# Sparse attention and gated feed-forward on one core: a first unit of 512 rows in the place of one of 384, with lent tiles, late mask copies and constant matmuls

## The chip, the core and the metric

The kernel runs on one NeuronCore of a Trainium2 chip. A core has five engines that run side by side: TensorE (PE: matmuls; PEld is its loading of weights), VectorE (DVE), ScalarE (ACT), GpSimd (POOL) and SyncE (SP, which here only issues DMA transfers). Sixteen DMA engines move data between HBM and the core's memory. Matmul results land in PSUM[...]; everything else lies in SBUF. The metric is the time in microseconds (us) of one execution on the device, as the median of several.

## The reference

Four batches of eight heads with 768 positions and 64 values a head pass a sparse causal attention. The keys are cut into 24 chunks of 32. For each query an upper bound of its score with each chunk is computed from the chunk's minimum and maximum; the six best chunks are kept. The attention's output, 3072 rows of 512, passes a feed-forward layer (FFN) with a sigmoid gate.

```python
ub = np.sum(np.maximum(q[:, :, :, None, :] * k_min[:, :, None, :, :], q[:, :, :, None, :] * k_max[:, :, None, :, :]), axis=-1)
ub = np.where(causal, ub, -1000000000.0)
top_chunks = np.argsort(ub, axis=-1)[..., -top_k:]
scores = scale * np.matmul(q, k.transpose(0, 1, 3, 2))
...
mask = sel & (pos[:, None] >= pos[None, :])
scores = np.where(mask, scores, -1000000000.0)
...
return np.matmul(attn, v)
# then, with x of 3072 x 512, w_gate and w_val 512 x 1536, w_out 1536 x 512:
gate = 1.0 / (1.0 + np.exp(-(x @ w_gate)))
val = x @ w_val
return gate * val @ w_out
```

## The kernel before

The rows are cut into 24 blocks of 128 (four batches of six). The first block of a batch sees at most four chunks, so all of them are kept and no choice is needed. A unit is a group of blocks that passes attention and FFN together. Each unit but the first is prepared (keys and queries turned, chunks chosen) and attended while PE also does the FFN of the unit before it.

```python
units = [
    Unit(0, [], [(0, 0), (1, 1), (2, 2)]),        # first blocks of batches 0, 1, 2
    Unit(1, [(0, 1), (0, 2), (0, 3)]),
    Unit(2, [(0, 4), (0, 5)], [(3, 2)]),          # and the first block of batch 3
    Unit(3, [(1, 1), (1, 2), (1, 3)]),
    ...
    Unit(7, [(3, 3), (3, 4), (3, 5)]),
]
```

A first block: its k and q are turned by PE (4 matmuls of 128x128 in f32 each), copied to f16, multiplied into scores, passed through exp on ACT, masked by a select on GpSimd, multiplied with the values, scaled and turned into `xT`, the FFN's input.

```python
def first(u, b, x, raw, base):
    for n in "kq":
        t = ps(f"{n}fT_{b}", "pr", [128, NP, 128])
        ...   # four transposes
        half[n] = Buf("np", f"{n}f16_{b}", [128, NP, 128], F16)
    ...
    val = Buf("np", f"vf_{b}", [128, H, D + 1], F16)
    att = [Buf("att", f"attf_{b}_{e}", [128, NP, 128], F16) for e in range(2)]
    ...   # scf (PE), expf (ACT), cmf (GpSimd select), pvf (PE), rzf and xf (DVE), xpsf (PE), xTf (DVE or ACT)
```

The FFN of a unit has twelve columns blocks `fb`. Each takes four matmuls for the gate, four for the value, a tanh on ACT (the sigmoid is made of it) and a product on DVE; then three row blocks of twelve output matmuls follow.

```python
def ffn(u, base, span):
    for fb in range(NFB):
        g = ps(f"g_{u.name}_{fb}", "ff", [128, T])      # T = 384
        w_ = ps(f"v_{u.name}_{fb}", "ff", [128, T])
        ...   # g: 4 matmuls, tanh on ACT; v: 4 matmuls, scalar_tensor_tensor on DVE
    for tb in range(3):
        ...   # o: 12 matmuls of 512 columns, a copy, a store
```

The FFN weights are loaded and cast to f16 by nine transfers issued by GpSimd (1 MB read each), the first pair after q of batch 1 has landed, the others after the last select of the first blocks:

```python
weights(0, -0.9, [(raw_f[1]["q"], 1)])
last = next(op for op in plan.ops if op.name == "cmf_2_1")
for i in range(1, 3):
    for op in weights(i, -0.5 + 0.2 * i, []):
        op.deps.append((last, False))
for i in range(3):
    weights_out(i, 0.3, []).deps.append((last, False))
```

A list scheduler inside the kernel (`Plan`) places every operation by a model of the engines, and the program is emitted in that order; each engine then runs its own instructions strictly in it. Constants in text (`NUDGES`, `LANDS`) steer it. They order instructions and are no waits on the chip.

Of the kernel before, what the change touches and what calls it, by code (L numbers as in the profile page):

```python
# [9 lines left out]
F16 = mybir.dt.float16  # L10
# [10 lines left out]
SHARED = {128: (0.145, 0.95), 256: (0.173, 0.90), 512: (0.22, 0.83), 768: (0.29, 0.78), 2048: (0.5, 0.5)}  # L21
SENT, LANDED = {SP: 700, POOL: 2700}, 1100
# [12 lines left out]
class Op:  # L35
    def __init__(self, name, engines, emit, prio, dma, rows, port):
        self.name, self.engines, self.emit, self.prio, self.dma = name, engines, emit, prio, dma
        self.rows, self.port = rows, port
        self.deps = []
        self.bufs = []  # L40
        self.start = self.done = self.engine = None

# [29 lines left out]
class Plan:  # L72
# [37 lines left out]
    def walk(self, land, prio=None, script=None, slow=1.0):  # L110
# [3 lines left out]
        line = {SP: 0.0, POOL: 0.0}  # L114
        port = {DVE: 0.0, POOL: 0.0}
        flight = []
# [4 lines left out]
        def inputs(op, e):  # L121
# [9 lines left out]
            for b in op.bufs:  # L131
                if b.kind == "ps":
                    for (other, r), done in seen.get(b, {}).items():
                        if other != e and r in op.rows:
                            t = max(t, done + HOP[e])
            if e == POOL:
# [28 lines left out]
        def place(op, e, s):  # L165
# [5 lines left out]
            if op.dma is not None:  # L171
                work = op.dma[0] * slow
                begin = max(line[e], s + SENT[e])
# [3 lines left out]
                if e == SP:  # L177
# [42 lines left out]
        while avail:  # L220
            best = None
            at = {}
            for op in avail:
# [3 lines left out]
                for e in op.engines:  # L227
                    at[op, e] = max(r, inputs(op, e))
# [27 lines left out]
    def landings(self, out, slow=1.0):  # L256

        queues = {SP: [], POOL: []}
        for op in out:
            if op.dma is not None:  # L260
                queues[op.engine].append([op.start + SENT[op.engine], op.dma[0] * slow, op])
# [3 lines left out]
        while queues[SP] or queues[POOL]:  # L265
# [5 lines left out]
            if len(on) == 2:  # L271
# [21 lines left out]
    def order(self):  # L293

        nudge = {n: int(x) for n, x in (w.rsplit(":", 1) for w in NUDGES.split())}
        lands = {n: float(x) for n, x in (w.rsplit(":", 1) for w in LANDS.split())}
        prio = {op: op.prio + nudge.get(op.name, 0) * 0.01 for op in self.ops}
# [7 lines left out]
ident:370 epat0:-92 epat:-143 kcr0:-70 kcr1:88 hq0:-119 hq1:74 ap0:168 v10:48 hkp000:102 hkp001:162 hkp010:1  # L305
hkp011:-53 ap1:113 v11:43 hkp100:139 hkp101:127 hkp110:-301 hkp111:-12 ident16:15 kf0_0:-159 kf1_0:-55 qf0_0:-66
qf1_0:-51 vf_0:27 kf0_1:-30 kf1_1:-16 qf0_1:-8 qf1_1:65 vf_1:10 kf0_2:24 kf1_2:41 qf0_2:-23 qf1_2:-11 vf_2:54
k0_u1:-125 k1_u1:-15 k2_u1:-44 k3_u1:35 q0_u1:-10 q1_u1:29 q2_u1:-4 q3_u1:38 v_0_1:-51 v_0_2:-11 v_0_3:24 kfT_0:99
kf16_0:-28 kxf0:60 kxf1:201 kcr_f:18 hkf0:348 hkf1:-115 qfT_0:94 qf16_0:-40 v16_0_0:238 scf_0:-96 expf_0_0:-210
# [998 lines left out]
```

The softmax here doesn't subtract the row's maximum and nothing guards it: scores larger than these inputs give would overflow.

## Time and profile before

| | |
|---|---|
| median of 3 executions | 294.98 us (293.96 to 295.21) |
| span of the profiled execution | 293.9 us |
| granted PE clock, mean | 0.988 |
| PE busy | 278.2 us, 95% |
| ACT, DVE, POOL busy | 195.8, 189.2, 92.5 us |
| HBM read, written | 30.67 MB, 6.29 MB |
| the chain that ended last | PE 78%, DMA 10%, DVE 4% |

The span is the time from the first to the last instruction of the profiled execution; it is about a microsecond shorter than the measured time. Matmuls overlap in PE's pipeline, so their busy times add up to more than the work; the time from one start to the next is the better measure of what a matmul costs. A wait is put down to the event that came last before the instruction could start.

### The profile page before, as it was taken

How to read it: one execution, taken by the hardware profiler on the slowest of the kernel's cores; microseconds unless marked ns; L12 is line 12 of the kernel's file. 1: busy time of each engine (PE TensorE's matmuls, PEld its weight loads, DVE VectorE, ACT ScalarE, POOL GpSimd, SP SyncE). 2: the span in 40 equal slices, each digit the busy share in tenths (PEclk: the TensorE clock that was granted, in tenths of full speed). 3: DMA queues.
4: the chain of work that ended last, by engine and by line, in shares of the span. 5: the costliest groups of instructions: out<-in, count | busy, mean ns of one | idle time of the engine just before them, and what ended most of it. 6: DMA issues, size and time to landing. Idle time of an engine off the chain costs nothing.

```text
span 293.9 us, 6954 instructions
## 1 busy us (share of the span) xinstructions
PE 278.2 (95%) x2656; PEld 176.7 (60%) x2656; DVE 189.2 (64%) x560; ACT 195.8 (67%) x398; POOL 92.5 (31%) x162
## 2 busy tenths in 40 slices
PE   2879998999989999999999999999999999999994
PEld 2645555767664566556666667676565557655651
DVE  8375883996999289999999899654134124432420
ACT  7674757977984879458889898886563466323321
POOL 6681314933652337013326954213000011000000
PEclk9977999999999999999999999999999999999999
DMA  7999999999967999399997300001100110011002
GB/s 165 218 249 216 197 197 235 220 146 166 184 100 90 203 188 184 67 215 152 142 210 145 111 3 3 0 2 39 71 2 1 50 60 0 2 38 71 0 15 95
DMA packets 123233, 32.69 MB, mean 111 GB/s; under 512 B 111424, under 2 KB 120128, under 8 KB 123200
## 3 DMA queue, kind: packets, MB, share of 16 engines
q1 hardware_dynamic: 118448, 27.53, 53.1%
q0 software_dynamic: 4752, 4.72, 9.5%
q8 instruction: 21, 0.34, 0.5%
q14 instruction: 12, 0.10, 0.1%
HBM read 30.67 MB, written 6.29 MB: 126 GB/s over the span
## 4 chain that ended last, share of the span: by engine, by line
PE 78%; DMA 10%; DVE 4%; SPq 2%; POOL 2%; ACT 1%; issue 1%; ACTq 0%; DVEq 0%
PE o_u L1168 20%; PE v_u L1146 18%; PE g_u L1146 18%; PE sc_u L1063 11%; DMA wo<-in_moe_w_out_dram 9%; PE pv_u L1096 6%; PE ube_u L1002 2%; SPq L742 2%; PE xps_u L1123 2%; DMA qf<-in_q_dram 1%; DVE qf_u L969 1%; DVE kcr L787 1%; DVE kt L953 1%; ACT attf L857 1%; PE qfT L815 1%
## 5 line engine op out<-in xcount | busy, mean ns | idle before, releaser
L1074 ACT ACTIVATE att_u<-sc_u 128x512 f16<-128x512 f32 (+3 forms) x184 | 88.0, 549 | 13.9 <-PE sc_u L1063 13.1
L1158 DVE SCALAR_TENSOR_TENSOR hg_u<-gate_u,v_u 128x384 f16<-128x384 f16 x96 | 51.8, 544 | 53.8 <-PE v_u L1146 37.0
L1146 PE MATMUL g_u<-xT_u,wg 128*128 128x384 f16 x384 | 79.3, 330 | 0.0
L1146 PE MATMUL v_u<-xT_u,wv 128*128 128x384 f16 x384 | 78.8, 328 | 0.3 <-DMA wv<-in_moe_w_val_dram 0.3
L1154 ACT ACTIVATE gate_u<-g_u 128x384 f16<-128x384 f32 x96 | 47.6, 495 | 39.1 <-DVE hg_u L1158 21.5
L1168 PE MATMUL o_u<-wo,hg_u 128*128 128x512 f16 x288 | 68.0, 379 | 1.1 <-DMA wo<-in_moe_w_out_dram 1.1
L1080 POOL TENSOR_SCALAR_AFFINE_SELECT att_u<-att_u 128x384 f16<-128x384 f16 (+1 forms) x56 | 28.4, 512 | 99.0 <-ACT att_u L1074 98.2
L1146 PEld LDWEIGHTS <-wv 128*128 128x128 f16 x384 | 36.8, 98 | 23.5 <-issue 0.8
L1146 PEld LDWEIGHTS <-wg 128*128 128x128 f16 x384 | 36.5, 99 | 21.8 <-issue 1.5
L1168 PEld LDWEIGHTS <-hg_u 128*128 128x128 f16 x288 | 27.1, 98 | 28.7 <-issue 1.5
L1177 ACT ACTIVATE osb_u<-o_u 128x512 f32<-128x512 f32 x20 | 12.1, 603 | 26.7 <-PE o_u L1168 25.0
L1096 PEld LDWEIGHTS <-att_u 128*128 128x128 f16 x640 | 25.5, 98 | 4.7
L1096 PE MATMUL pv_u<-v,att_u 128*128 128x65 f16 x640 | 28.0, 193 | 0.0
L1063 PE MATMUL sc_u<-hqo,hko 128*128 128x128 f16 (+2 forms) x220 | 27.8, 243 | 0.1
L1063 PE MATMUL sc_u<-hqe,hke 128*128 128x128 f16 (+2 forms) x220 | 27.1, 243 | 0.2 <-ACT att_u L1074 0.2
L1063 PEld LDWEIGHTS <-hke 128*128 128x128 f16 x220 | 16.8, 98 | 5.7 <-issue 1.2
L779 POOL CAST v<-v 128x512 f16<-128x512 f32 x23 | 13.9, 619 | 19.2 <-DMA v<-in_v_dram 18.9
L1063 PEld LDWEIGHTS <-hko 128*128 128x128 f16 x220 | 16.3, 98 | 4.8 <-issue 0.2
L576 DVE COPY xT_u<-xps_u 128x384 f16<-128x384 f16 (+1 forms) x17 | 5.7, 338 | 14.4 <-PE xps_u L1123 14.3
L1115 DVE TENSOR_TENSOR x_u<-pv_u,rz_u 128x384 f16<-128x384 f32 (+1 forms) x28 | 14.5, 523 | 0.4
L1025 DVE MAX8 mx_u<-ubn_u 128x8 f32<-128x8 f32 (+16 forms) x152 | 12.4, 156 | 0.1
L787 DVE TRANSPOSE_TENSOR_REDUCE kcr<-k 128x24 f32<-128x768 f32 x12 | 11.2, 941 | 0.8 <-DMA k<-in_k_dram 0.8
(119 smaller groups left out, 306.9 us busy)
## 6 DMA issues: line engine op xcount, KB each, us to landing
out_dram<-osb_u SPq DMA_DIRECT2D x24, 256.0 KB, 2.4
v<-in_v_dram SPq DMA_DIRECT2D x23, 256.0 KB, 5.0
k<-in_k_dram SPq DMA_DIRECT2D x12, 384.0 KB, 6.1
q<-in_q_dram SPq DMA_DIRECT2D x12, 384.0 KB, 6.8
wg<-in_moe_w_gate_dram POOLq DMA_DIRECT2D x3, 512.0 KB, 10.2
wv<-in_moe_w_val_dram POOLq DMA_DIRECT2D x3, 512.0 KB, 12.8
wo<-in_moe_w_out_dram POOLq DMA_DIRECT2D x3, 512.0 KB, 23.3
kf<-in_k_dram SPq DMA_DIRECT2D x8, 128.0 KB, 3.6
```

The source lines that it names most:

```text
L779: plan.add(f"v16_{b}_{ib}", {POOL: pool(H * D)}, lambda e: nc.gpsimd.tensor_copy(v16[b % 2][:, ib, :, 0:D], at(t)), reads=[t], writes=[("v ...
L787: plan.add(f"kx{m}_{name}_{p}", {DVE: dve(size)}, lambda e, m=m, op=op: nc.vector.tensor_reduce(out=outs[m](), in_=src(), op=op, axis=AX.X ...
L1025: nc.vector.max(at(mx)[:, e_, j, :], at(ubn)[:, e_, j, 0:max(8, u.seen[j])])
L1063: nc.tensor.matmul(at(t)[:, o:o + 128 * m], hk[b % 2][e_][:, p, 128 * jb:128 * jb + 128], hq[u.side][e_][:, p, 128 * x:128 * (x + m)], sta ...
L1074: plan.add(f"exp_{u.name}_{h}_{y}", {ACT: act(n)}, lambda e, t=t, att=att, b0=b0, n=n: nc.scalar.activation(at(att)[:, b0:b0 + n], at(t), ...
L1080: nc.gpsimd.affine_select(out=dv, in_=dv, compare_op=ALU.is_ge, fill=0.0, base=0, pattern=[[0, u.m], [1, 128]], channel_multiplier=-1)
L1096: nc.tensor.matmul(at(pv)[:, last, x, :], at(att)[:, c:c + 128], v16[b % 2][:, jb, h, :], start=(jb == 0), stop=(jb == ib))
L1115: plan.add(f"x_{u.name}_{p}", {DVE: dve(u.t)}, lambda e: nc.vector.tensor_tensor(at(x_).rearrange("p a (e d) -> p e a d", e=2), at(pv)[:, ...
L1146: nc.tensor.matmul(at(t), w16[:, c, 128 * fb:128 * fb + 128], at(u.xt)[:, c, :], start=(c == 0), stop=(c == 3))
L1154: plan.add(f"tanh_{u.name}_{fb}", {ACT: act(T)}, lambda e, g=g, gate=gate: nc.scalar.activation(at(gate), at(g), AF.Tanh, scale=0.5), read ...
L1158: plan.add(f"hg_{u.name}_{fb}", {DVE: dve(T)}, lambda e, w_=w_, gate=gate, hg=hg: nc.vector.scalar_tensor_tensor(at(hg), at(gate), 1.0, at ...
L1168: nc.tensor.matmul(at(o), at(hgs[fc])[:, 128 * tb:128 * tb + 128], wo16[:, fc, :], start=(fc == 0), stop=(fc == NFB - 1))
```

## The change

Unit 0 takes the first blocks of all four batches, 512 rows, and unit 2 has only its two blocks of batch 0, 256 rows. The purpose is to have more FFN work at hand while the weights are still landing, and the first block of batch 3 out of the way of the later attention. What goes with it:

- The small tiles of the first blocks (k and q in f16, values, attention) are lent: they lie in the key, query and value buffers of later batches (`hk[1]`, `hq[0]`, `v16[1]`), and in the buffers `qm` and `qf` for the raw data of batches 2 and 3. The operations that write those buffers for their own purpose wait for the last use.
- The mask copies into `hk` (`hkp`) are held back until the first gate product of unit 0, or of unit 1 for the second buffer.
- Constant matmuls (identity times identity, about 55) are put into PE's gaps in the front, so that PE's clock stays up. Their result is not used.
- The FFN's matmuls take as many columns as the unit has rows (512, 256 or 384). In unit 0 four gate products come before the first four value products; in the others one.
- The weight transfers are chained one after another and wait for q of batch 2 instead of q of batch 1.
- The chosen chunks' tile `ubn` shares the one buffer of `qm`.
- An early exp on ACT loads its table; the scheduler's model is refined and has a new list `HOLDS`, which only moves operations in the order; all of `NUDGES` and `LANDS` is new.

```diff
-        Unit(0, [], [(0, 0), (1, 1), (2, 2)]),
+        Unit(0, [], [(0, 0), (1, 1), (2, 2), (3, 3)]),
         Unit(1, [(0, 1), (0, 2), (0, 3)]),
-        Unit(2, [(0, 4), (0, 5)], [(3, 2)]),
+        Unit(2, [(0, 4), (0, 5)]),
...
-                      reads=[epat], writes=[("hkp", i, e_, p) for p in range(o, NP, 2)], prio=0.3 + 0.2 * i, port=True)
+                      reads=[epat], writes=[("hkp", i, e_, p) for p in range(o, NP, 2)], prio=0.7 + 0.8 * i, port=True)
+                later.append((f"hkp{i}{e_}{o}", "g_u0_0" if i == 0 else "g_u1_0"))
...
-            half[n] = Buf("np", f"{n}f16_{b}", [128, NP, 128], F16)
+            half[n] = Lent(hk[1][b // 2], (0, 1024, 0, 1544)[b] + 512 * "kq".index(n), [NP, 128])
...
-            val = Buf("np", f"vf_{b}", [128, H, D + 1], F16)
+            val = Lent(*((None, None), (hk[1][0], 2048), (hk[1][1], 1024), (hq[0][0], 0))[b], [H, D + 1])
...
-        att = [Buf("att", f"attf_{b}_{e}", [128, NP, 128], F16) for e in range(2)]
+        att = [Lent(v16[1], 1024 * b - 1024 + 512 * e, [NP, 128]) if b else Buf("att", f"attf_{b}_{e}", [128, NP, 128], F16)
+               for e in range(2)]
...
-        ubn = Buf("ubn", f"ubn_{u.name}", [128, 2, u.nb, 32])
+        ubn = Buf("qm", f"ubn_{u.name}", [128, 2, u.nb, 32])
...
-            g = ps(f"g_{u.name}_{fb}", "ff", [128, T])
+            g = ps(f"g_{u.name}_{fb}", "ff", [128, u.rows])
...
+        first_ = 4 if u.i == 0 else 1
+        for fb in range(first_):
+            gated(fb)
+        for fb in range(first_):
+            valued(fb)
+        for fb in range(first_, NFB):
+            gated(fb)
+            valued(fb)
...
-        for tb in range(3):
+        for tb in range(u.rows // 128):
...
+    warm = ps("warm", "wm", [128, 128])
+    for name, n in {"": 10, "kfT_0": 4, "qfT_0": 3, "kfT_1": 3, "qfT_1": 3, "scf_1": 3, "pvf_0_1": 3, "kfT_2": 3, "qfT_2": 3, "pvf_1_1": 4, "scf_2": 3, "xpsf_1_1": 5, "pvf_2_1": 3, "g_u0_3": 2, "pvf_3_1": 3}.items():
+        for i in range(n):
+            op = plan.add(f"warm{name}_{i}", pe(213, 170), lambda e: nc.tensor.matmul(at(warm), ident32, ident32, start=True, stop=True),
+                          reads=["ident32"], writes=[warm], prio=1.7)
+            wake.append((op, name))
...
-    weights(0, -0.9, [(raw_f[1]["q"], 1)])
-    last = next(op for op in plan.ops if op.name == "cmf_2_1")
-    for i in range(1, 3):
-        for op in weights(i, -0.5 + 0.2 * i, []):
-            op.deps.append((last, False))
+    gate = [raw_f[2]["q"][1][1]]
+    weights(0, 4, -1.2, gate)
+    weights(4, 8, -1.6, [])
+    weights(8, 12, -1.6, [])
     for i in range(3):
-        weights_out(i, 0.3, []).deps.append((last, False))
+        weights_out(i, -0.6, []).deps.append((half["last"], None))
...
-    first(units[2], 3, 2, raw_f[3], 2.0)
```

## The prediction

> **What bounds the kernel now.** I read the page's engine table first, then its forty slices, then the stretches, the PE timeline of the first 50 us, the waits of PE and the tail.
>
> ```profile
> PE 278.2 (95%) x2656; PEld 176.7 (60%) x2656; DVE 189.2 (64%) x560; ACT 195.8 (67%) x398; POOL 92.5 (31%) x162
> ...
> PE   2879998999989999999999999999999999999994
> ...
> PEclk9977999999999999999999999999999999999999
> DMA  7999999999967999399997300001100110011002
> ```
>
> PE is the bound from about a tenth of the span on; the front is different: PE partly idle, its clock at 7 in slices three and four, and the DMA engines full until about 80 us. So the front has to be read by itself. In the stretches (columns: length, then busy time of PE, PEld, DVE, ACT, POOL, granted PE clock, DMA share, GB/s):
>
> ```profile
> 4.95:12.00 7.05, 5.21 (x27) 3.87 (x28) 4.09 (x8) 5.09 (x8) 3.90 (x6) 1.00 1.33 229
> ...
> 18.80:21.60 2.80, 2.13 (x13) 1.49 (x11) 1.42 (x5) 1.49 (x4) 2.80 (x5) 0.50 1.15 279
> 21.60:25.60 4.00, 4.00 (x16) 1.97 (x14) 2.78 (x7) 2.00 (x6) 1.30 (x2) 0.54 1.19 230
> ...
> 48.10:289.90 241.80, 240.42 (x2388) 153.15 (x2387) 157.40 (x463) 163.36 (x336) 70.88 (x121) 1.00 0.54 92
> 289.90:293.90 4.00, 0.13 (x1) 0.00 (x0) 0.00 (x0) 0.60 (x1) 0.00 (x0) 1.00 0.17 66
> ```
>
> Until 21.6 us PE only does small work for three first blocks. Then the first feed-forward (FFN) starts at half clock. From 48.1 us PE is never seen waiting long, and 4.0 us of tail follow. The PE timeline and waits show the rest:
>
> ```profile
> 18.55 0.40 PE L866 MATMUL pvf<-vf,attf 128*128 128x65 f16 x4 [1.06 <-POOL attf L859]
> ...
> 21.61 1.49 PE L1146 MATMUL g_u<-xT_u,wg 128*128 128x384 f16 x4
> 22.89 1.49 PE L1146 MATMUL v_u<-xT_u,wv 128*128 128x384 f16 x4
> 24.17 1.38 PE L1146 MATMUL g_u<-xT_u,wg 128*128 128x384 f16 x4
> 25.39 0.81 PE L1146 MATMUL v_u<-xT_u,wv 128*128 128x384 f16 x4
> ```
>
> ```profile
> PE o_u L1168 <- DMA wo<-in_moe_w_out_dram: 1.1, 1, 1.1
> ...
> PE v_u L1146 <- DMA wv<-in_moe_w_val_dram: 0.3, 1, 0.3
> ```
>
> Start to start, a product of four matmuls takes 1.28 us at 22 us and 0.65 us later (26.04, 26.69, 27.34 in the same timeline). The last weights issued at 22.1 us land at 48.05, which the 1.1 us wait shows.
>
> So the span splits into 21.6 (before the first gate product) + 268.3 (to the end of the last output product near 289.9) + 4.0 (tail). How much of the 268.3 is work? From start-to-start times: 768 gate and value matmuls of 384 columns x 0.1625 = 124.8; 288 output matmuls x 0.216 = 62.1; scores, 81,920 columns at 0.417 ns plus 440 x 2.5 ns = 35.2; 640 values matmuls x 0.030 = 19.4; 80 transposes back x 0.056 = 4.5; 31 key and query transposes x 0.115 = 3.6; chunk bounds, 77,824 columns at 0.105 ns (sixteen of 320 columns in 0.54 us), 8.2; the first block of batch 3, done inside this stretch, 1.6. Together 259.4. Of the 8.9 us left, 1.8 is the half clock (three products at 3.78 instead of 1.95), 1.4 the two DMA waits, 1.3 other waits listed, about 4.4 small gaps. That is all that can be won after 21.6 us.
>
> **What the Trainium skill says.** "TensorE: Matmul & The Clock Gate", Part 1, says the array runs at half clock unless it was busy in a preceding window of about 3.4 us. The trace agrees: 0.50 to 0.54 granted between 18.8 and 25.6 us, after a stretch (15.4 to 18.8) with 2.08 us of PE busy in 3.40. The same page's section "Wait — 56ns, not 53.3ns?" gives a matmul a fixed 2.5 ns besides columns over 2.4 GHz; the trace agrees: 384 columns at 0.65/4 = 162.5 ns. So a 512-row product saves nothing per row worth speaking of. "DMA: Bandwidth & Descriptors", section "Issuing engines are not separate DMA queues", says that transfers of all issuing engines share the same 16 DMA engines; the trace agrees: 200 to 280 GB/s for both queues together, DMA share over 1 from 5 to 45 us. Bytes put ahead delay those behind.
>
> **The change part by part.**
>
> *Fourth first block in the front.* It takes 1.6 us of PE out of the saturated part, and puts 0.75 MB of k, q and v ahead of the second unit's k and q and of the weights. At about 0.22 MB/us that is some 3.5 us. In the built program's order of instructions, the fourth block's last k and q are the eighteenth transfer of SyncE. Before, fifteen issues took from 0.81 to 9.8 us, 0.6 each, and landed about 4 us later: 0.8 + 17 x 0.6 + 4 = 15.0 us.
>
> *When the first FFN can start.* It now needs all four blocks. In the new order GpSimd has the nine weight issues and four mask selects in a row, with the fourth block's two selects last. An issue is 0.76 us, a select 0.62. The first issue waits for the second half of batch 2's q (fourteenth transfer, about 12.6 us) and for the selects of batch 1, say 13.3 us. So the last select ends at 13.3 + 9 x 0.76 + 4 x 0.62 = 22.6. Before, 2.1 us passed from the end of the last select (18.5) to the last copy into xT (20.6); one transpose group of unit 1 stands between, 0.4. Estimate: first gate product at 25.1 us instead of 21.6: **+3.5**.
>
> *512 rows in unit 0, 256 in unit 2.* Columns are the same in sum (512 + 256 = 2 x 384), matmuls the same in number: **0** in PE work. A product grows to 0.87 us, and a pair of weight tiles, 2 x 3.4 us apart, then feeds 8 x 0.87 = 7.0 us of PE: the FFN needs weights no faster than they land. The weight stream starts about 3 to 4 us later (wo last near 51 us instead of 48), but FFN work alone lasts 24 x 0.87 = 20.9 from 25.1, and with unit 1's preparation and scores PE has work to about 51. I take both DMA waits as gone: **-1.4**.
>
> *Constant matmuls.* About 55 products of the identity in PE's gaps keep the clock up. They save the half-clock excess, **-1.8**; seven of them stand behind the first gate product and cost 7 x 0.11 = **+0.8**. Those before lie in idle time.
>
> *Four gates before four values, in unit 0.* Value weights are needed 3.5 us later; counted in the waits already.
>
> *Mask copies held back.* Eight copies of 64x1536, 0.5 to 1.5 us each, leave DVE and ACT's first 8 us, four of them for the second key buffer to about 70 us and later. DVE and ACT then have less in the front; DVE is at nine tenths in most slices from 75 to 160 us, but unit 3's attention comes later by unit 0's extra rows, so I count **0**.
>
> *Lent tiles, ubn in the place of qm.* The first blocks' small tiles lie in buffers that are written again only after use. The qm of a unit must wait for the mask choice of the one before. Both **0**, with a risk.
>
> Sum: span 293.9 + 3.5 - 1.6 - 1.4 - 1.8 + 0.8 = 293.4. The median before is 1.0 above the profiled span, so 294.4. The order of all instructions is tuned anew; of about 4.4 us of small gaps I give it 1, and half as much back to the q risk below: **294.0**.
>
> **Rivals.**
> 1. *The second unit's q becomes the wait.* PE takes its work in program order, and two q transpose groups of unit 1 stand between the value products of unit 0, due at about 32 us. Before, the last q went through at 32.1 us with no wait, with 0.75 MB less ahead of it; it could land at 35. For: DMA full to 45 us. Against: part of the delay falls on the weights instead. It costs 0 to 3 us: up to 297.
> 2. *The front ends earlier than I think.* With a warm clock each transpose group of a first block falls from 0.9 to about 0.45 us, and fewer DVE and ACT copies are in the way; if GpSimd's issues do not hold the last selects, the first gate product is at 23 us. For: the wait of 1.06 us for a select. Against: nine issues ahead of the last selects. Time: 292.
> 3. *The clock falls anyway.* If the constant matmuls leave one 3.4 us window too empty, up to 3.4 us run at half clock, 1.7 lost: 296.
> 4. *The tuned order is worth more.* If the small gaps and waits behind 48 us shrink by 3 of their 5 us: 291.
>
> **Range and chances.** Four shifts of 1.5 to 3 us, hardly linked, about 294.0: 289.5 to 298.5. Faster by over 2% would need 289.1 or less, rivals 2 and 4 together; slower by over 2% needs 300.9, a wait not seen here. Chances 0.10, 0.82, 0.08; below 295 is a little likelier than above.
>
> **What would show it.** The first gate product of 512 columns at 25 us (right within 1); PE clock 1.00 from 12 us on; no wait for wo and wv, and a wait before unit 1's q transposes under 1 us; gate products 0.87 us start to start; the stretch from first gate product to last output product near 264 instead of 268.3; the same tail of 4.0. I am wrong if the first gate product comes before 23 or after 27.5, if a wait of over 2 us appears in 25 to 50 us, or if PE gets gaps between 75 and 160 us where DVE is full.

## The result, and the profile after

The changed kernel takes 298.37 us (median of 4, 297.63 to 299.81) where the kernel before takes 295.10 beside it (293.96 to 295.22): 1.0126 times, 95% interval 1.0078 to 1.0174. The forecast was 294.0 us, a little faster than before; the change costs 3.3 us. A later set of runs gave 298.82 against 295.41 us, 1.0124 (1.0094 to 1.0154).

First the page of the changed kernel: busy time and instructions of the engines, two rows of the forty slices, the chain that ended last.

```profile
PE 287.9 (97%) x2766; PEld 189.3 (63%) x2766; DVE 187.1 (63%) x555; ACT 198.2 (66%) x406; POOL 96.3 (32%) x160
...
PE   7989899999999999999999999999999999999994
...
PEclk9999999999999999999999999999999999999999
DMA  7999999999999999917990990002000110001002
...
PE 65%; DMA 11%; DVE 10%; SPq 8%; issue 2%; POOL 1%; ACT 1%; DVEq 0%; ACTq 0%; POOLq 0%
```

The 7s in the clock's row are gone, so the constant matmuls do what they are for. PE has 110 instructions more and looks busier (97%), yet the span is 298.1 us instead of 293.9: busy is not the same as useful. And the chain that ended last has more of SyncE's issues (8% instead of 2%) and of DVE (10% instead of 4%) in it. The stretches (columns as before) tell where to look:

```profile
12.00:27.53 15.53, 13.70 (x146) 12.41 (x146) 8.71 (x27) 9.15 (x20) 11.63 (x18) 1.00 1.20 219
27.53:43.10 15.57, 13.98 (x103) 7.71 (x101) 11.53 (x26) 8.70 (x19) 2.01 (x4) 1.00 1.20 212
55.00:294.10 239.10, 238.05 (x2383) 153.91 (x2381) 154.72 (x455) 166.78 (x343) 75.25 (x119) 1.00 0.60 88
294.10:298.10 4.00, 0.08 (x1) 0.00 (x0) 0.00 (x0) 0.60 (x1) 0.00 (x0) 0.87 0.17 66
```

From 55 us on PE is saturated as before, and the tail is 4.0 us as before. The first 43 us, now at full clock, are what is left. PE's timeline there (start, length, line, what; in brackets the wait and what ended it):

```profile
27.53 2.75 PE L1270 MATMUL g_u<-xT_u,wg 128*128 128x512 f16 x12
...
34.03 0.55 PE L1023 MATMUL kT_u<-ident,kn_u 128*128 128x128 f32 x3 [0.54 <-POOL kn_u L681]
...
35.92 0.55 PE L1023 MATMUL qT_u<-ident,qn_u 128*128 128x128 f32 x3 [0.47 <-ACT qn_u L677]
...
37.91 0.52 PE L1023 MATMUL qT_u<-ident,qn_u 128*128 128x128 f32 x3 [0.58 <-DVE qn_u L679]
...
41.16 0.45 PE L1130 MATMUL ube_u<-qf_u,kcr 64*32 64x320 f32 x1
```

In the kernel before, the same last q transposes and bounds stood here:

```profile
32.10 0.55 PE L901 MATMUL qT_u<-ident,qn_u 128*128 128x128 f32 x3
...
36.47 0.45 PE L1002 MATMUL ube_u<-qf_u,kcr 64*32 64x320 f32 x1
```

The first gate product starts at 27.53 instead of 21.61 us, and unit 1's transposes are waited for three times. The chunk bounds of unit 1 (`ube`) start at 41.16 instead of 36.47. A second trace of the changed kernel (e16 below) has the gate product at 27.27 and the bounds at 40.14, so two traces of one kernel can be a microsecond apart. The chain of waits in the first 60 us names the cause of the last of these waits:

```profile
20.87 16.32 DMA kq_u<-in_q_dram
37.21 0.56 DVE qn_u L679
37.91 0.52 PE qT_u L1023 x3
...
...
42.47 0.86 PE warm L1340 x6
```

SyncE issues unit 1's last q at 20.87 us, it takes 16.3 us to land, at 37.2, and DVE and PE stand behind it. In the kernel before it was issued at 14.54 and landed 16.9 us later, at 31.4 (KB each, us from issue to landing):

```profile
kq_u<-in_q_dram SPq DMA_DIRECT2D x1, 192.0 KB, 16.9
```

Constant matmuls (`warm`) lie on the chain too. The late gate product has another cause, seen on ACT and GpSimd:

```profile
17.00 0.37 ACT L677 COPY xT_u<-xpsf 128x256 f16<-128x256 f16 x1
21.22 0.51 ACT L677 COPY kn_u<-kq_u 128x384 f32<-128x384 f32 x1 [3.84 <-DMA kq_u<-in_k_dram]
21.64 1.08 ACT L979 ACTIVATE v<-scf 128x512 f16<-128x512 f32 x2
```

```profile
22.48 0.74 POOL L838 DMA_DIRECT2D wo<-in_moe_w_out_dram  x1 [1.53 <-DMA wg<-in_moe_w_gate_dram]
23.23 1.23 POOL L981 TENSOR_SCALAR_AFFINE_SELECT v<-v 128x512 f16<-128x512 f16 x2
```

ACT's next instruction at 17.4 is a copy of unit 1's keys, which land only at 21.2; the fourth block's two exps stand behind it. GpSimd then has its ninth weight issue to do, which waits 1.53 us for the first weight's landing, and only then the fourth block's selects. Now what SyncE's queue (q1) and the weights' queue (q0) moved (packets, MB, share of 16 engines). First the changed kernel between 13 and 15 us, with no weights in flight:

```profile
q1 hardware_dynamic: 1711, 0.43, 128.9%
```

Then between 21 and 28 us, beside the weights, before and after:

```profile
q0 software_dynamic: 910, 0.91, 76.8%
q1 hardware_dynamic: 1143, 0.70, 41.6%
```

```profile
q0 software_dynamic: 946, 0.94, 78.8%
q1 hardware_dynamic: 937, 0.68, 39.5%
```

Alone, SyncE's queue moves 0.21 MB/us, and in this time the fourth block's loads go through: by 17 us the queue has moved 3.14 MB, which are the four first blocks (4 x 0.79); 2.36 MB, three of them, are moved by 12.6 us in both kernels. Beside the weights the queue has 0.10 MB/us in both kernels, of 0.23 in all, and unit 1's keys and queries (eight transfers, 1.57 MB) go at this rate: its last seven, 1.38 MB in some 16 us, at 0.086. (The profile counts a weight's bytes as they are written, in f16; read is twice as much, 9.4 MB of the 30.67 in all.)

"DMA: Bandwidth & Descriptors" of the Trainium skill, section "Queues, rings and completion order", says that each DMA engine takes its queues in turn, packet by packet. The trace agrees: in these 7 us of the changed kernel the two queues move 946 and 937 packets. So what a queue gets beside another follows from the size of its packets. From 37 to 41 us, when SyncE's packets have 260 bytes on average (0.16 MB in 621) instead of 730, its queue has 0.04 MB/us.

### The profile page after: what moved, and what is told of

Same layout as the page of the kernel before. It is cut to its first block, busy times and chain, and to the rows that moved or that the text cites. A ratio compares the mean times of both kernels' runs of the same rounds, so it can differ in the third digit from the quotient of the medians.

```text
span 298.1 us, 7171 instructions
## 1 busy us (share of the span) xinstructions
PE 287.9 (97%) x2766; PEld 189.3 (63%) x2766; DVE 187.1 (63%) x555; ACT 198.2 (66%) x406; POOL 96.3 (32%) x160
## 3 DMA queue, kind: packets, MB, share of 16 engines
q1 hardware_dynamic: 118448, 27.53, 58.3%
HBM read 30.67 MB, written 6.29 MB: 124 GB/s over the span
## 4 chain that ended last, share of the span: by engine, by line
PE 65%; DMA 11%; DVE 10%; SPq 8%; issue 2%; POOL 1%; ACT 1%; DVEq 0%; ACTq 0%; POOLq 0%
PE v_u L1270 16%; PE g_u L1270 16%; PE o_u L1309 15%; PE sc_u L1191 9%; DMA kq_u<-in_q_dram 5%; PE pv_u L1224 5%; DMA k<-in_k_dram 3%; SPq L862 3%; PE ube_u L1130 2%; SPq L873 2%; DMA q<-in_q_dram 2%; SPq L883 2%; DVE qf_u L1097 2%; DVE kcr L907 1%; DVE kt L1081 1%
## 5 line engine op out<-in xcount | busy, mean ns | idle before, releaser
L1202 ACT ACTIVATE att_u<-sc_u 128x512 f16<-128x512 f32 (+3 forms) x184 | 90.0, 546 | 19.9 <-PE sc_u L1191 19.3
L1290 DVE SCALAR_TENSOR_TENSOR hg_u<-gate_u,v_u 128x384 f16<-128x384 f16 (+2 forms) x96 | 51.9, 545 | 54.6 <-PE v_u L1270 40.5
L1270 PE MATMUL v_u<-xT_u,wv 128*128 128x384 f16 (+2 forms) x384 | 78.1, 326 | 0.0
L1270 PE MATMUL g_u<-xT_u,wg 128*128 128x384 f16 (+2 forms) x384 | 77.8, 326 | 0.0
L1283 ACT ACTIVATE gate_u<-g_u 128x384 f16<-128x384 f32 (+2 forms) x96 | 46.8, 494 | 28.8 <-PE g_u L1270 16.1
L1208 POOL TENSOR_SCALAR_AFFINE_SELECT att_u<-att_u 128x384 f16<-128x384 f16 (+1 forms) x56 | 29.5, 530 | 107.8 <-ACT att_u L1202 107.5
L1270 PEld LDWEIGHTS <-wv 128*128 128x128 f16 x384 | 36.2, 98 | 20.8 <-DVE x_u L1243 0.2
L1224 PEld LDWEIGHTS <-att_u 128*128 128x128 f16 x640 | 24.6, 97 | 7.0 <-POOL att_u L1208 1.2
L1224 PE MATMUL pv_u<-v,att_u 128*128 128x65 f16 x640 | 27.5, 194 | 0.8 <-POOL att_u L1208 0.3
L1191 PE MATMUL sc_u<-hqe,hke 128*128 128x128 f16 (+2 forms) x220 | 27.6, 243 | 0.0
L1191 PE MATMUL sc_u<-hqo,hko 128*128 128x128 f16 (+2 forms) x220 | 27.4, 244 | 0.1
L1318 ACT ACTIVATE osb_u<-o_u 128x512 f32<-128x512 f32 x24 | 14.3, 597 | 18.1 <-PE o_u L1309 17.9
L1191 PEld LDWEIGHTS <-hke 128*128 128x128 f16 x220 | 17.4, 98 | 8.0 <-issue 0.6
L1340 PE MATMUL warm<-ident 128*128 128x128 f32 x110 | 18.8, 307 | 1.4 <-POOL ident masks.py:199 1.4
L1340 PEld LDWEIGHTS warm<-ident 128*128 128x128 f32 x110 | 16.0, 212 | 2.4 <-POOL ident masks.py:199 1.4
## 6 DMA issues: line engine op xcount, KB each, us to landing
out_dram<-osb_u SPq DMA_DIRECT2D x24, 256.0 KB, 2.3
v<-in_v_dram SPq DMA_DIRECT2D x23, 256.0 KB, 5.0
```

Of the source, the lines that this page charges most:

```text
L1191: nc.tensor.matmul(at(t)[:, o:o + 128 * m], hk[b % 2][e_][:, p, 128 * jb:128 * jb + 128], hq[u.side][e_][:, p, 128 * x:128 * (x + m)], sta ...
L1202: plan.add(f"exp_{u.name}_{h}_{y}", {ACT: act(n)}, lambda e, t=t, att=att, b0=b0, n=n: nc.scalar.activation(at(att)[:, b0:b0 + n], at(t), ...
L1208: nc.gpsimd.affine_select(out=dv, in_=dv, compare_op=ALU.is_ge, fill=0.0, base=0, pattern=[[0, u.m], [1, 128]], channel_multiplier=-1)
L1224: nc.tensor.matmul(at(pv)[:, last, x, :], at(att)[:, c:c + 128], v16[b % 2][:, jb, h, :], start=(jb == 0), stop=(jb == ib))
L1270: nc.tensor.matmul(at(t), w16[:, c, 128 * fb:128 * fb + 128], at(u.xt)[:, c, :], start=(c == 0), stop=(c == 3))
L1283: plan.add(f"tanh_{u.name}_{fb}", {ACT: act(u.rows)}, lambda e: nc.scalar.activation(at(gate), at(g), AF.Tanh, scale=0.5), reads=[g], writ ...
```

## The experiments

Theory A: the fourth block's 0.79 MB of loads stand ahead of unit 1's keys and queries in SyncE's queue, and these move at the rate that the weights leave; the late queries set the bounds, the bounds set the masks, and the masks the scores. B: the late first gate product costs directly. C: what the front gains or loses, the fixed order of the later work changes again. For every kernel the start of `ube` is given beside its time:

| kernel | first gate product | first `ube` | profiled span | median | ratio to before (95%) |
|---|---|---|---|---|---|
| before | 21.6 | 36.5 | 293.9 | 295.1 | 1 |
| changed | 27.5 | 41.2 | 298.1 | 298.37 | 1.0126 (1.0078 to 1.0174) |
| e1 fourth block first | 24.7 | 41.0 | 297.5 | 298.82 | 1.0106 (1.0059 to 1.0153) |
| e2 FFN ahead | 27.6 | 44.7 | 300.2 | 301.94 | 1.0214 (1.0164 to 1.0264) |
| e3 both orders | 24.5 | 45.7 | 301.3 | 302.40 | 1.0228 (1.0186 to 1.0271) |
| e4 no constant matmuls | 26.7 | 39.5 | 297.1 | 298.81 | 1.0102 (1.0074 to 1.0129) |
| e5 no fourth loads | 29.6 | 40.8 | 297.9 | 297.88 | 1.0084 (1.0049 to 1.0119) |
| e6 before, with the loads | 30.6 | 45.4 | 301.6 | 302.88 | 1.0218 (1.0165 to 1.0270) |
| e7 order by landing | 24.5 | 44.4 | 300.2 | 302.46 | 1.0229 (1.0196 to 1.0262) |
| e8 the same, no constant | 23.5 | 44.7 | 300.3 | 302.01 | 1.0208 (1.0174 to 1.0242) |
| e9 no loads, block first | 24.5 | 40.2 | 296.8 | 298.90 | 1.0130 (1.0100 to 1.0159) |
| e10 weights spaced | 26.8 | 38.1 | 294.1 | 296.91 | 1.0073 (1.0039 to 1.0107) |
| e11 spaced, block first | 24.7 | 45.3 | 303.2 | 303.89 | 1.0302 (1.0265 to 1.0339) |
| e12 value weight late too | 24.7 | 46.4 | 304.4 | 305.73 | 1.0363 (1.0333 to 1.0393) |
| e13 spaced, fewer constant | 26.7 | 37.1 | 295.6 | 297.05 | 1.0062 (1.0039 to 1.0084) |
| e14 spaced, few constant | 25.5 | 37.6 | 296.6 | 297.32 | 1.0075 (1.0053 to 1.0098) |
| e15 that, block first | 26.8 | 41.6 | 297.5 | 297.52 | 1.0081 (1.0060 to 1.0103) |
| e16 changed, again | 27.3 | 40.1 | 296.3 | 298.82 | 1.0124 (1.0094 to 1.0154) |
| e17 spaced, again | 27.4 | 38.7 | 295.7 | 297.73 | 1.0079 (1.0051 to 1.0107) |

In all 19 traces 255.5 to 259.0 us pass from the first `ube` to the end of the span, while `ube` itself lies between 36.5 and 46.4; from the first gate product to the end it is 267.3 to 279.7. So a microsecond by which the bounds are later is, within some 2 us, a microsecond at the end, and the first gate product tells much less.

The profile is one execution; its span is 1.7 us shorter than the time of that execution, which can lie 1 to 2 us off the median, so spans a microsecond apart tell nothing and medians decide. All but e5, e6 and e9 compute everything, and those say what they leave out or add. Each edit moves, drops or adds operations in the finished order, with a helper that puts named operations behind another one:

```diff
-    for op in plan.order():
+    order = plan.order()
+    def behind(names, anchor):
+        names = names.split()
+        group = [op for op in order if op.name in names]
+        rest = [op for op in order if op.name not in names]
+        i = next(i for i, op in enumerate(rest) if op.name == anchor) + 1
+        order[:] = rest[:i] + group + rest[i:]
+    ...   # the calls of the experiment
+    for op in order:
         op.emit(op.engine)
```

**e1, e2, e3: the orders.** e1 puts five weight issues behind the fourth block's selects and unit 1's keys behind the first gate products; e2 pulls FFN products ahead of unit 1's last queries and its bounds; e3 does both.

```diff
+    behind("wg8 wv8 wo1 wo2 wo0", "cmf_3_0")                          # e1, e3
+    behind("kn_u1_3 kT_u1_3 kx0_u1_3 kx1_u1_3 kt_u1_3 ...", "g_u0_0")   # e1, e3; u1_1 behind g_u0_1, u1_0 behind tanh_u0_2
+    behind("qn_u1_2 qT_u1_2 qf_u1_2 ...", "hg_u0_4")                  # e2, e3; kn_u1_2 ... behind hg_u0_1
+    behind("qn_u1_3 qT_u1_3 qf_u1_3 ...", "hg_u0_5")                  # e2, e3
+    behind("ub_u1 ... mx1_u1 mx0_u1 ap1_u1 ap0_u1", "hg_u0_6")        # e2, e3
```

> Changed kernel (298.4 us), with the fourth first block put ahead of unit 1's keys: in program order, the copies and transposes of unit 1's first three key groups come behind the first gate products, and the last five weight issues of GpSimd come behind the fourth block's two selects. Theory A (late q: PE, ACT and GpSimd wait in a fixed order for unit 1's k and q, whose last landing at 37.2 us sets when unit 1 can be prepared): the first gate product moves from 27.5 to about 23 us, but PE then waits the longer for unit 1's k and q between the value products, and the time falls by 0 to 1.5 us only: 297 to 298.4. Theory B (late start: the FFN's start sets the end, what comes after is as before): the first gate product at 23 us and the time falls by as much, about 4.5 us: 294.

> Changed kernel, with unit 1's last key group and its last two query groups, and the choice of its chunks, moved behind further products of unit 0's FFN in program order, so that no engine reaches them before they have landed. Theory A (PE waits in order for q landing at 35 to 37 us): the first gate product stays at 27.5 us, the lost time between 27.5 and 43 us (15.6 us for about 11.3 us of work) falls by 2.5 to 4 us, time 294.5 to 296. Theory B (the start sets the end): no change, 298 within 1. Rival C (unit 1's mask choice becomes the wait, since it comes later): a gap of PE at 45 to 52 us and time 298 or more.

> Both reorderings together. Theory A: start at about 23 us and no waits for q until about 38 us; the gains add up to 6 to 9 us, time 290 to 292.5. Theory B: 294, as for the first alone. Rival C (weights set the pace): PE waits for the value weights at 26, 33 and 40 us instead, time 293 to 295.

e1's timeline of PE shows an earlier gate product and no earlier bounds:

```profile
24.66 1.02 PE L1270 MATMUL g_u<-xT_u,wg 128*128 128x512 f16 x4
...
27.60 1.04 PE L1270 MATMUL g_u<-xT_u,wg 128*128 128x512 f16 x4 [1.58 <-DVE kt_u L679]
...
40.99 0.45 PE L1130 MATMUL ube_u<-qf_u,kcr 64*32 64x320 f32 x1
```

The gate product came 2.6 to 2.9 us earlier than in the two traces of the changed kernel; the bounds (40.99 against 41.16 and 40.14) and the time did not: B alone falls. In e2 and e3 PE does more FFN first, the bounds come 3.5 to 4.5 us later, and the scores then wait for their masked queries (2.25 us in e3):

```profile
51.85 0.66 PE L1191 MATMUL sc_u<-hqe,hke 128*128 128x256 f16 x6 [2.25 <-ACT hqe L677]
```

So in these orders more FFN rows at hand, which is what the first unit of 512 rows is for, are of no use: the bounds are what PE needs next, and PE delays them itself when it does something else.

**e4: no constant matmuls.** All operations whose names begin with `warm` are left out; nothing uses their results.

```diff
+        if not op.name.startswith("warm"):
             op.emit(op.engine)
```

> Changed kernel without any of the constant matmuls; all else in the same order. If they do what they are meant to: PE clock at half [...] between 15 and 31 us, the first gate products at 1.7 us start to start instead of 0.87, and the time 1.5 to 3 us longer, 300 to 301.5. If they only stand in the way (each 0.11 to 0.21 us in PE's order ahead of the fourth block's work): the start comes up to 1 us earlier, and the time is 297.5 to 298.4. Under theory A the half clock would be hidden in the wait for q: 298 within 1.

```profile
26.71 5.19 PE L1270 MATMUL g_u<-xT_u,wg 128*128 128x512 f16 x12
...
39.51 0.45 PE L1130 MATMUL ube_u<-qf_u,kcr 64*32 64x320 f32 x1
```

Three gate products last 5.19 us instead of 2.75 (half clock) and the bounds still start 0.6 to 1.6 us earlier than in the two traces of the changed kernel; the time is the same. What the clock wins, the constant matmuls' own PE time seems to take back; the runs show only the sum.

**e5, e6: the loads alone.** e5 leaves out the fourth block's five loads and computes that block from the third's tiles. e6 adds those five loads to the kernel before, behind its last first-block load, into a buffer that nobody reads.

```diff
+    for n in "kqv":                                                   # e5
+        raw_f[3][n] = (raw_f[2][n][0], raw_f[3][n][1])                # and kf0_3 kf1_3 qf0_3 qf1_3 vf_3 are not emitted
```

```diff
+        if op.name == "vf_2":                                         # e6, kernel before
+            extra = rot.tile([128, 3, H, D], F32, tag=f"qf{slot}", name="extra")
+            ...   # nc.sync.dma_start: k and q of batch 3 in two halves each, v
```

> Changed kernel (298.4 us) without the five transfers (0.79 MB) of the fourth first block; that block is computed from the k, q and v of the third, so its 128 rows of output are those of other inputs, and all the work of the engines stays. Theory D (the front is bound by bytes: SyncE's transfers land in turn beside the weights, and 0.79 MB ahead push unit 1's k and q and with them the whole front): unit 1's last q lands about 3.5 us earlier (33.5 instead of 37.2), the chunk bounds at 37.5 to 38 instead of 41.2, the time falls by 2.5 to 4 us, to 294.5 to 296. Rival (order of instructions alone, GpSimd's issues and selects): the bounds come at most 1 us earlier, 297.5 to 298.4.

> Kernel before (295.5 us) with the same 0.79 MB of k, q and v of batch 3's first block loaded into an unused buffer right after the third block's v, and read by nobody: only bytes are added. Theory D: unit 1's k and q land about 3.5 us later, PE waits for its transposes, and the time rises by 2 to 3.5 us, to 297.5 to 299, that is nearly as slow as the changed kernel. Rival (bytes are hidden behind PE's work, the changed kernel is slow for its order): rise under 1 us.

e6 costs 7.4 us, more than twice what was expected. SyncE and PE in it:

```profile
15.69 7.45 SPq L753 DMA_DIRECT2D kq_u<-in_k_dram  x3
```

```profile
25.82 0.90 PE L901 MATMUL kT_u<-ident,kn_u 128*128 128x128 f32 x3 [9.67 <-ACT kn_u L574]
```

The first keys of unit 1 are not there until 25 us, and in the order of the kernel before everything on ACT and PE stands behind them for 9.67 us. That the loads alone cost several microseconds is shown; the size belongs to that order, and to the weights, which here are already under way beside the added loads (1.03 MB of weights between 13 and 21 us; in the changed kernel they begin at 16). In e5 no query is waited for any more, but a second limit takes over, and the time falls by less than the runs can tell:

```profile
24.78 0.30 PE L988 MATMUL pvf<-hqe,v 128*128 128x65 f16 x4 [2.31 <-POOL v L981]
```

The fourth block's selects still stand behind the ninth weight issue on GpSimd, and the gate product is at 29.55.

**e7, e8: an order by landing.** The operations of 24 to 45 us sorted by when their data land in the changed kernel, with e1's weight move; e7 leaves out the constant matmuls behind the gate products, e8 all of them.

```diff
+    behind("wg8 wv8 wo1 wo2 wo0", "cmf_3_0")
+    behind(late, "xTf_3_1")      # late: g_u0_0 g_u0_1 tanh_u0_0 kn_u1_3 ... g_u0_8 ... hg_u0_8, then sorted as listed
```

> Changed kernel with the instructions from the first gate product to the chunk bounds put in the order in which their data landed in the changed kernel's trace, the last five weight issues behind the fourth block's selects as before, two PSUM banks exchanged, and the constant matmuls behind the first gate product left out. If order alone is at fault (theory A): first gate product at 24.5 us, PE busy to the end of the front, the chunk bounds at about 40, time 293 to 295. Theory D (bytes): the bounds cannot come before about 39.5 since the last q lands at 37, the FFN only fills the time up to there; a gain of 1 to 3 us, time 295.5 to 297.5.

> As the last one, without any constant matmul. The clock is then at half for one or two windows at the first gate products: theory says 1 to 2.5 us longer than the last one; if the constant matmuls cost as much as they win (as their removal from the changed kernel, within 0.5 us of it, says), the same within 1 us.

Both are about 4 us slower than the changed kernel: bounds at 44 to 45 us, a 2.42 us wait of the scores in e7. My guess at a better order for all engines was worse than the kernel's.

**e9: both limits of e5 and e1 at once.** The edits of e1 and e5 together.

> Leaves out the five loads of the fourth batch's first block (0.79 MB; that block is computed from the third batch's tiles) and also puts five of the weight issues and three blocks of unit 1's keys behind the fourth block. Theory A (two limits lie side by side in the changed kernel, the late landing of unit 1's queries and the late fourth block; either alone hides the other): with both gone the first gate product starts at about 24.7 us, unit 1's queries are not waited for by more than 0.5 us, the chunk bounds (ube) start at 36 to 38 instead of 41.2, and the time is 293 to 295 us. Rival C (the front is not what costs; the tuned order of the body loses the same time later): bounds at 36 to 38 and still 297 us or more. Rival D (GpSimd and ScalarE hold unit 1 back in any case): bounds at 40 or later.

Bounds at 40.2 and 298.9 us: two limits side by side were not all. In this order ACT's `kn_u` and GpSimd's copies of unit 1 come after the gate products (PE waits 1.58 us for `kt_u` at 27.4), so this run cannot separate the loads from the order any more. It fits rival D of its text.

**e10, e11, e12: weights out of the way.** e10 changes only the places of seven weight issues on GpSimd; e11 adds e1's moves of the keys; e12 also holds the first value weight back.

```diff
+    behind("wg4", "cmf_3_0")               # e12: "wv0 wg4"
+    behind("wv4", "kn_u1_0")
+    behind("wg8 wv8", "hk0_u1_1")
+    behind("wo1", "hk1_u1_0")
+    behind("wo2 wo0", "kn_u1_2")
```

> Complete computation. Of the nine weight issues only the first gate and the first value weight stay early; the other seven are spread behind the fourth block's selects and GpSimd's copies for unit 1. Theory A (SyncE's loads move at 0.084 MB/us beside the weights and at 0.22 MB/us alone): some 3 us without weights in flight move 0.4 MB more, so unit 1's last queries land at 32 to 34 us instead of 37.2, the first gate product starts at about 25, bounds at 37 to 39, time 294.5 to 296.5 us. Rival B (the loads are as slow without weights beside them): last queries land at 36 to 37, time 297.5 to 298.5. Rival C: bounds early, time still 297 or more, or a wait for a weight (second gate weight) appears on TensorE and takes the gain.

> The spaced weights, and three blocks of unit 1's keys behind the first gate products. Theory A: first gate product at about 24.5, bounds at 36 to 39, time 294 to 296 us; as the spaced weights alone or up to 1 us better. Rival C: no better than 297.

> As the spaced weights with the blocks of keys behind, and the first value weight held back too, so that one weight alone lies beside unit 1's loads until about 23 us. Theory A: queries land another 1 to 2 us earlier (30 to 32 us), bounds at 35 to 38, time 293.5 to 296 us, unless TensorE waits for the first value weight: then that wait, 1 to 3 us, gives it back and the time is 296 to 298.

e10's queues between 21 and 28 us, and its PE:

```profile
q1 hardware_dynamic: 2802, 1.54, 79.4%
q0 software_dynamic: 461, 0.45, 38.4%
```

```profile
34.84 0.49 PE L1023 MATMUL qT_u<-ident,qn_u 128*128 128x128 f32 x3
...
38.07 0.45 PE L1130 MATMUL ube_u<-qf_u,kcr 64*32 64x320 f32 x1
```

SyncE's queue moves 1.54 MB in the stretch in which it moved 0.68: with fewer weights in flight it has 0.22 MB/us instead of 0.10. The last q transposes start at 34.84 with no wait, and the bounds at 38.07, 3.1 and 2.1 us earlier than in the two traces of the changed kernel. That is theory A's mechanism, by an edit that moves nothing but weight issues. The edit also takes seven issues from ahead of the fourth block's selects; e17 below tells the two apart. e11 and e12 missed: with the keys moved, the issues anchored behind key copies slid back as well, and PE waits for a value weight, 2.6 us in e11 and 3.4 in e12:

```profile
PE v_u L1270 <- DMA wv<-in_moe_w_val_dram: 2.6, 1, 2.6
```

**e13, e14, e15: what then holds the front.** e13 is e10 without the seven constant matmuls behind the first gate product; e14 also without those after about 22 us; e15 is e14 with the fourth block ahead of unit 1's keys on ACT and PE.

```diff
+    order[:] = [op for op in order if not op.name.startswith(("warmg_u0_3", "warmpvf_2_1_1", "warmpvf_2_1_2", "warmpvf_3_1"))]   # e13
+    # e14, e15: ("warmg_u0_3", "warmpvf_2_1", "warmpvf_3_1", "warmxpsf_1_1", "warmscf_2")
+    behind("kn_u1_3", "xTf_2_0")           # e15; kT_u1_3 behind pvf_3_0, kn_u1_1 behind xTf_3_0, kT_u1_1 behind g_u0_0, kT_u1_0 behind g_u0_1
```

> The spaced weights (complete computation), without the seven constant matmuls that stand behind the first gate product (14 instructions of 0.115 us). With the weights spaced no wait for unit 1's queries is left and TensorE's own order sets the bounds at 38.1 us; if so (theory A, continued) these 1.6 us come off: bounds at 36.5, first gate product unchanged at 26.8, time 295.3 us (the spaced weights alone: 296.9). Rival: they stood in slack, bounds stay near 38 because a copy or a load of unit 1 arrives then, and the time is 296.5 to 297.5.

> As the last, and the 26 instructions of constant matmuls between about 22 and 26.8 us left out too. The chain of waits of the spaced weights counts 16 of them (1.9 us) before the first gate product. Theory A: first gate product at about 25, bounds at 35 to 36, time 293.5 to 295 us, if the clock stays near full. Rival: the fourth block and the keys set that start, the gate product stays above 26 and the time equals the last one's; or the clock is down at the first gate products and gives 1 us back.

> As the last, and the fourth block ahead of unit 1's keys on ScalarE and TensorE. Its scores are ready at 17.4 us but its exponentials wait until 21.2 behind a copy of keys that land late. Theory A: exponentials at about 17.5, first gate product at 21 to 24, and then TensorE waits for unit 1's keys and queries again (landing near 33): bounds at 34 to 36, time 292.5 to 294.5 us, at best 1 us under the last one. Rival: an order untuned elsewhere costs as much as in the three earlier reorderings, and the time is 296 or more.

e13's bounds came at 37.1, 1.0 earlier than e10's, and its time did not move; from the bounds to the end are 258.5 us, against 256.0 in e10. PE later in e13:

```profile
53.11 0.31 PE L1224 MATMUL pv_u<-v,att_u 128*128 128x65 f16 x5 [0.68 <-POOL v L899]
...
85.39 0.38 PE L1191 MATMUL sc_u<-hqo,hko 128*128 128x256 f16 x2 [1.36 <-DVE xT_u L679]
```

PE now arrives ahead of GpSimd's value casts and DVE's copies and waits there: theory C, seen for the first time with a name. In e14 the gate product is at 25.52, but the clock is down there (twelve matmuls take 4.18 us instead of 2.75), and another wait follows at 106.85 us:

```profile
25.52 4.18 PE L1270 MATMUL g_u<-xT_u,wg 128*128 128x512 f16 x12
...
106.85 0.42 PE L1224 MATMUL pv_u<-v,att_u 128*128 128x65 f16 x8 [1.52 <-POOL att_u L1208]
```

In e15 the exps run at 17.47, and the fourth block then waits for its own values, which SyncE loads last of all:

```profile
20.82 0.62 ACT L677 CAST hqe<-kqvf 128x512 f16<-128x512 f32 x1 [2.26 <-DMA kqvf<-in_v_dram]
```

Its gate product is at 26.8 all the same. The late loads of the fourth block itself are a third limit on that start.

**e16, e17: changed and spaced side by side.** The unedited changed kernel and e10, on one chip.

> The changed kernel once more, so that it stands on the same chip and beside the same runs of the kernel before as the spaced weights. All theories: about 298.4 us, 1.010 to 1.016 times the kernel before.

> The spaced weights once more, beside the changed kernel. Theory A (the shared transfer rate is part of the cost): 296.5 to 297.2 us, at least 1 us under the changed kernel in the same call. Rival (the first difference was one between chips or hours): the two within 0.5 us of each other.

298.82 and 297.73 us: 1.1 us apart, in the direction of theory A. The last q transposes and the bounds, first in e16, then in e17:

```profile
36.89 0.52 PE L1023 MATMUL qT_u<-ident,qn_u 128*128 128x128 f32 x3 [0.81 <-DVE qn_u L679]
...
40.14 0.45 PE L1130 MATMUL ube_u<-qf_u,kcr 64*32 64x320 f32 x1
```

```profile
35.46 0.49 PE L1023 MATMUL qT_u<-ident,qn_u 128*128 128x128 f32 x3
...
38.69 0.45 PE L1130 MATMUL ube_u<-qf_u,kcr 64*32 64x320 f32 x1
```

The first gate product does not come earlier in e17 (27.44 against 27.27), although no more than two weight issues stand ahead of the selects there; the wait for q is gone and the bounds come 1.45 us earlier. So it is the loads, and not an earlier start, that the spaced weights help. Against the kernel before, whose bounds are at 36.47, e17's bounds are 2.2 and e16's 3.7 us later, and the times 2.3 and 3.4 us longer.

The intervals of the two ratios to before still overlap slightly (1.0094 to 1.0154 and 1.0051 to 1.0107). Both pairs together, ten executions of the changed kernel and eleven of the spaced one, each over the mean of the kernel before beside it, differ by 1.5 us (0.6 to 2.3, an estimate from their single times). So of the whole cost of 3.4 us some 1.1 to 1.5 us come back when the weights stand aside. No version here beats the kernel before.

## Why the prediction was wrong, point by point

**The step that failed: unit 1's loads.** The prediction has them some 3.5 us late, lets part of this fall "on the weights instead", and gives the wait 0.5 us in the sum. It divided 0.75 MB by about 0.22 MB/us, the rate of both queues together. For the fourth block's own loads that is about right: they go before the weights, and four blocks are through at 17 us where three were at 12.6. What failed is the step from there to unit 1. Its keys and queries go beside the weights, packet for packet, at 0.10 MB/us. In the kernel before, some of them went before the weights began (at 13 us), and between 20 and 22 us, when few weights were in flight, SyncE's queue moved 0.47 MB; in the changed kernel hardly any go before, and it is 0.18 in the same 2 us. The first keys are copied at 21.2 us instead of 15.4, and the last q lands at 37.2 (36.2 in e16) instead of 31.4, where the text had 35. This cost more than a wait: PE waits for unit 1's k and q for 0.54 + 0.47 + 0.58 = 1.6 us (1.1 in e16) against the 0.5 of the sum, and the late first keys also hold the fourth block's exps on ACT, and so the first gate product. Rival 1 was the right one and was under-weighted; its cap of 297 was 1.4 us under the result. e10 and e17 confirm the mechanism for the queries; without that wait 1.1 to 1.5 us come back.

**First gate product at 25.1, +3.5.** It was 27.53 (27.27 in e16): +5.9 or +5.7, and the last select ends at 24.5 instead of 22.6. The text saw one holder, nine issues and selects on GpSimd. There are two, which end within 0.5 us of each other: the ninth weight issue, which waits 1.53 us for the first weight to land and is done at 23.2, and ACT's copy of late keys ahead of the fourth block's exps (a wait of 3.84 us), which are done at 22.7. In e17 seven of the nine issues stand behind the selects, and the copy alone, with a wait of 4.43 us, holds the start at 27.44; in e5 the exps are early and the ninth issue waits 2.20 us. So the term was too small by 2.4 and its mechanism half seen; e1 shows that pulling this start back by 2.9 us gives nothing by itself.

**Constant matmuls, +0.8.** Each f32 product is two PE instructions of 0.115 us, so the seven behind the gate product are 14 and cost 1.6 us; six of the instructions are on the chain at 42.47. **Half clock, -1.8**: right, the granted clock is at 1.00 until the tail, and the first gate products take 0.86 us each. Together the two bring nothing (e4).

**Fourth block out of the saturated part, -1.4 for weight waits.** Right: among PE's waits none is for wo or wv any more, and a gate product of unit 0 takes 0.86 us from start to start (the forecast: 0.87). **The tail**: 4.0 us, right.

**Stretch from first gate product to last output product: 264.** It was 266.6 (27.53 to 294.1). The 2.3 us over the sum's 264.3 are the 1.6 of q and k waits and the extra 0.8 of the constant matmuls, within 0.1. With the +2.4 of the gate product that makes the difference between the span of 293.4 in the text and 298.1. This trace is of the slowest of four executions; in e16's, of the fastest of six, with a span of 296.3, the stretch is 265.0, and the late start is the larger part, 2.2 of 2.9 us. This split is bookkeeping along one trace, and it does not say what each part is worth when taken away alone: e1, e4, e5 and e13 each take one away (e13 from the spaced weights), and none gains more than the runs can tell.

**Mask copies, lent tiles, `ubn`, 0.** In the changed kernel's trace no wait of PE after 43 us is over 0.3 us, so none of them shows as a cost there. In the front four mask copies hold DVE from 27.75 to 29.80 us, right behind the first gate product, and PE is not seen waiting for DVE in that time. None of these parts was taken out alone. **The tuned order, -1 for gaps.** Not seen. Where the front was improved most (e13), PE met DVE and GpSimd later, and 1.36 and 0.68 us went into new waits.

**What stays open.** With the weights spaced, about 2 us remain over the kernel before (297.73 against 295.41). In e17 the gate product is again at 27.44 and the bounds at 38.7, 2.2 us later than before; e13 and e14 show that bounds at 37.1 and 37.6 do not lower the time, because the later order gives it back. These 2.2 us stand beside a first gate product that is 5.8 us late, but no run here brought both the start and the loads back to where they were before, so how they come about is argued from the traces and not shown. Whether an order tuned as long as that of the kernel before, for this start, would bring the 2 us back was not tried.

The range held, by 0.1 us (289.5 to 298.5 with 298.37 measured), and the time stayed within 2%; the direction was wrong.

## What to carry to other kernels

When two queues share the DMA engines, ask which transfers will be in flight together. Bytes that go alone cost bytes over the full rate; an urgent load that goes beside another full queue costs its bytes over its own share, here one of its packets for one of the other's. Ask of more work at hand whether it is the work that the next stage waits for: here PE had FFN to do, but the bounds of the second unit set the masks, and these the scores. And an instruction for late data placed ahead of work on early data in an engine's fixed order passes its delay on to that work, however idle the engine seems: here 3.84 us on ACT.

## What the runs showed of the hardware that was not expected

- Two full queues moved equal numbers of packets: 946 and 937 between 21 and 28 us in the changed kernel. SyncE's queue had 0.68 MB of it, and 1.54 MB in the same 7 us when the weights were spaced; the total rose from 1.62 to 1.99 MB as well.
- The ninth weight issue on GpSimd waited for the landing of the first (1.53 us in the changed kernel, 0.73 in e16, 2.20 in e5), as though eight were the most that may be under way; whether the chip or the program's own semaphores set this was not tested. In the kernel with e6's loads three SyncE issues took 7.45 us instead of 2.15.
- Keeping the clock up with constant f32 matmuls costs two instructions of 0.115 us each, 110 in this kernel; with fewer of them, in e14, the gate products fell to half clock again (4.18 instead of 2.75 us for twelve matmuls).
- The record of the granted clock reads 1.00 between 4.95 and 12 us in the kernel before, though four f32 transposes of a first block take 1.09 us at 7.86 there, and 0.60 us at 7.86 in the changed kernel, where constant matmuls go before them.
